# A mixture of experts whose line of experts becomes straight code for one shape, with its first branch a quarter block later

## The chip, the cores and the metric

The kernel runs on one core of a Trainium2 chip. The metric is the device time of one execution in microseconds (us), the median of several runs. TensorE (PE) multiplies, VectorE (DVE) and ScalarE (ACT) move and transform tiles, GpSimd (POOL) starts the indirect transfers (gathers and scatters of rows), and SyncE (SP) starts the plain ones.

## What is computed

Attention with pooled keys and values gives 2304 rows of 512; a dense layer (512 to 2048, square of relu, 2048 to 512) follows; then a layer of 8 experts, which the change is about. Each row goes to the expert with its largest logit:

```python
logits = x @ w_gate
expert_idx = np.argmax(logits, axis=1)
logits_s = logits - logits.max(-1, keepdims=True)
probs = np.exp(logits_s)
probs /= probs.sum(-1, keepdims=True) + 1e-09
gate_w = probs[np.arange(N), expert_idx]
...
h = np.maximum(np.einsum('ecd,edf->ecf', disp, w1), 0.0)
y = np.einsum('ecf,efd->ecd', h, w2)
...
out[i] = gate_w[i] * y[expert_idx[i], pos[i]]
```

Here `disp[e]` holds the rows of expert e, in order, up to its capacity of 576.

## The kernel before

Attention, dense layer and router run in chunks under a written order. Matmuls take float32 as a high and a low part, so a product is three matmuls (high by high, high by low, low by high). The rows of an expert are counted in half blocks of 64 (`nh`), and the experts are sorted by that count, largest first; position r in that order, not the expert's number, names a stage. For this input the counts are 9, 9, 8, 1, 1, 0, 0, 0. All later work hangs on these counts, which are known only on the chip, so each engine reads them from a table (`regs`) into a register and branches on it.

An expert's work is cut into passes. A `pair` takes two blocks of 128 rows: 8 hidden blocks (L1307), then for each block of rows an output block of 24 matmuls (`out_of`, `gb`, L1276), in four quarters of 6 matmuls with a `hook` after each, and then `finish` (ACT scales the rows by their gate, L1254, and POOL scatters them to the output, L1265). A `trio` adds a half block whose high and low parts are stacked (`gb2`, L1282). A `small` pass takes one half block, stacked too: 16 matmuls to the rows `hs[0]`, `hs[1]` (L1414), which ACT (L1419) and DVE (L1421) copy out, 16 to transpose them (L1426), 16 for the output (L1435), and `finish2` (ACT copy L1259, DVE add L1260, ACT scale L1261, scatter L1265). The hooks carry what other engines do for the next pass: the gathers of its rows (`next_rows`, POOL L859), their transposes (`y_trans`, L887, or `y_half`, L904 for one half block; both with an ACT copy and a DVE subtraction), and `w_split`, which turns a 512 KB pair of weight tiles in a staging buffer into high and low parts (ACT L231, DVE L232) and has SP load the next one.

`finish` always goes through one tile `ysb`: ACT may write it only when the scatter before has read it. In `small(1)`, the first small pass, `hs[1]` is that same tile; the tile of `finish2` is `hs[1]` of the second small pass.

The first expert's first pass (`second`) is cut: its first output block runs, then all engines branch on R_LINE (`If` at L1644), and the second output block comes behind the branch in either arm. R_LINE and R_LAST (how many large and small experts follow) are written by 12 small DVE operations in `line_index`. In the arm that this input takes come `trio(0)` and `line(1)`. `line(r)` runs the passes of expert r, a trio or a pair first (`If` at L1578), then a pair; then it branches at L1588 (is there another expert than the last two) and L1589 (is it a large one: `line(r+1)`, or a small one: `smalls(r+1)`). Both branches have joins at which all engines wait for their own work only. `last_two` is two small passes. The order of instructions on PE, DVE and ACT is that of the code. During the last pair of `line`, the third large expert's, `y_trans` 0 to 2 prepare the next rows for either case: whole blocks, and `parted` a half block.

```python
with tc.If(val(regs, R_LAST, 0, NLAST) > (r + 2) // 2):
    with tc.If(halves(r + 1) > 6, preferred_fallthrough_block=False) as on:
        line(r + 1)
    with on.Else():
        smalls(r + 1)
```

Of the kernel before, what the change touches and what calls it, by code (L numbers as in the profile page):

```python
# [26 lines left out]
E = 8  # L27
# [16 lines left out]
R_LAST = R_LINE + 1  # L44
LINE = 4
NLAST = 3
# [153 lines left out]
def tile_kernel(ctx: ExitStack, tc: tile.TileContext, q, k, v, w_in, w_out, w_gate, w1, w2, cap, gate_rows, consts, out):  # L200
# [681 lines left out]
    def y_trans(t=0, then=None):  # L882
# [8 lines left out]
        if then:  # L891
            then(ps)

    def parted(ps):

        for i, t in enumerate(yc):
            nc.scalar.copy(out=t[:, :, 0], in_=ps[:, 2 * i:2 * i + 2, 0:HP])
            nc.vector.tensor_tensor(out=t[:, :, 1], in0=ps[:, 2 * i:2 * i + 2, 0:HP], in1=f(t[:, :, 0]), op=ALU.subtract)

    def y_half():  # L900
        gate_of(0)
        ps = pg.tile([P, KD, HP], F32, tag="g", name="yTs")
        for kk in range(KD):
            nc.tensor.transpose(ps[:, kk, :], got(0)[:HP, kk * P:(kk + 1) * P], ident[:HP, :HP])  # L904
        parted(ps)
# [29 lines left out]
    def early_plan():  # L935
# [3 lines left out]
        def rooms():  # L939
# [10 lines left out]
            st["regs"] = one("regs", [1, R_LAST + 1], I32)  # L950
# [26 lines left out]
    def finalize():  # L977
# [47 lines left out]
        st["nh"], st["cmp"], st["last"] = res[:, 2, 0:E, 0], cmp, ni[:, 0:1]  # L1025

    def line_index():


        nh, least, n, last = st["nh"], st["cmp"], st["ep"][2], st["last"]  # L1030
        for i, x in enumerate((7.0, 2.0, 1.0)):
            nc.vector.tensor_single_scalar(out=least[:, i], in_=nh, scalar=x, op=ALU.is_ge)
        nc.vector.tensor_reduce(out=n, in_=least[:, 0:3], axis=AX.X, op=ALU.add)
        nc.vector.scalar_tensor_tensor(out=last, in0=n[:, 0:1], scalar=2.0, in1=n[:, 2:3], op0=ALU.add, op1=ALU.max)
        nc.vector.tensor_single_scalar(out=regs[:, R_LAST:R_LAST + 1], in_=last, scalar=1, op=ALU.arith_shift_right)
        nc.vector.tensor_tensor(out=n[:, 1:2], in0=n[:, 1:2], in1=n[:, 0:1], op=ALU.is_equal)
        for src, x, op in (
            (nh[:, 0:1], 9.0, ALU.is_equal), (nh[:, 1:2], 9.0, ALU.is_le), (nh[:, 1:2], 7.0, ALU.is_ge),
            (n[:, 2:3], float(2 * NLAST + 1), ALU.is_le),
        ):  # L1040
            nc.vector.scalar_tensor_tensor(out=n[:, 1:2], in0=src, scalar=x, in1=n[:, 1:2], op0=op, op1=ALU.mult)
        nc.vector.scalar_tensor_tensor(
            out=regs[:, R_LINE:R_LINE + 1], in0=st["regse"][:, 2:3], scalar=1.0, in1=n[:, 1:2], op0=ALU.is_ge, op1=ALU.mult
        )
# [192 lines left out]
    yc = [gp.tile([P, 2, 2, HP], F32R, tag="r", name=f"yc{i}", bufs=2) for i in range(2)]  # L1237
    xh, xl = ([gp.tile([P, F2], F32R, tag=tag, name=f"{tag}_e{i}", bufs=2) for i in range(2)] for tag in ("xh", "xl"))
# [18 lines left out]
    def finish2(po, t, sidx, gate):  # L1257
        ot = st["yg2"][:, 0:DM]
        nc.scalar.copy(out=ot[:HP], in_=po[HP:])  # L1259
        nc.vector.tensor_tensor(out=ot[:HP], in0=po[:HP], in1=ot[:HP], op=ALU.add)  # L1260
        nc.scalar.activation(out=ot[:HP], in_=ot[:HP], func=AF.Copy, scale=gate[:HP, t:t + 1])  # L1261
        put(ot, t, sidx, HP)
# [24 lines left out]
    def pair(slot, hooks, extra=0, cut=False):  # L1287
# [39 lines left out]
        if extra:  # L1327
            po = pp.tile([P, 512], F32, tag="y0", name="po2")
            for i in range(4):
                gb2(w, hx, (2 * i, 2 * i + 1), po)  # L1330
                hook(16 + i)
            finish2(po, 2, *sg)
# [9 lines left out]
    def single(slot, hooks):  # L1342
# [44 lines left out]
        po = pp.tile([P, 512], F32, tag="y0", name="po")  # L1387
# [9 lines left out]
    def small(slot, hooks):  # L1397
# [33 lines left out]
        po = pp.tile([P, 512], F32, tag="y0", name="po")  # L1431
# [8 lines left out]
        finish2(po, 0, *sg)  # L1440
# [133 lines left out]
    def line(r):  # L1574


        now = splits(r + 1, {h: [i for i in range(16) if SPLITS[i] == h] for h in range(16)} if r == 1 else W_REST)
        with tc.If(halves(r) > 8, preferred_fallthrough_block=False) as half:  # L1578
            run(trio, r, 0, at=0, extra=now, third=4)
        with half.Else():  # L1580
            run(pair, r, 0, extra=now)
# [4 lines left out]
        if r == LINE:  # L1586
            return
        with tc.If(val(regs, R_LAST, 0, NLAST) > (r + 2) // 2):  # L1588
            with tc.If(halves(r + 1) > 6, preferred_fallthrough_block=False) as on:  # L1589
                line(r + 1)  # L1590
            with on.Else():
                smalls(r + 1)

    def smalls(r):

        small(r % 2, merged(
            {0: [next_rows(r + 1, 1)], 5: [y_half]},
            splits(r + 1, {1: (12, 13), 2: (14, 15)}),
            splits(r + 2, {3: (0, 2), 4: (4, 6, 1), 5: (3, 5), 6: (7, 8, 9), 8: (10, 11)}),
        ))  # L1600
        if r + 2 < 2 * NLAST:
            with tc.If(val(regs, R_LAST, 0, NLAST) > (r + 2) // 2):
                smalls(r + 1)

    def last_two():

        def rows():
            x = val(regs, R_LAST, 0, NLAST, DVE)
            fetch(nc.values_load(regs[0:1, bass.ds(x * (2 * NU) + (2 * E - 1), 1)], engines=DVE, min_val=0, max_val=E * NJ - 1), 1)

        small(1, merged({0: [rows], 5: [y_half]}, {
            h: [lambda i=i: w_split(0, i, None, 0)] for h, i in ((1, 12), (2, 13), (3, 14), (4, 15))
        }))
        small(0, {})
# [28 lines left out]
    with ordered(ET.DVE, ET.Activation):  # L1643
        with tc.If(val(regs, R_LINE, 0, 1) > 0, preferred_fallthrough_block=False) as on:  # L1644
            second()
            run(trio, 0, 1, True, 1, 3, extra={0: [lambda: w_load(regs, 1)]}, third=4)
            line(1)
            last_two()
        with on.Else():
            second()  # L1650
            rest()
# [73 lines left out]
```

## Time and profile before

| What | Value |
|---|---|
| Median of 3 runs | 724.53 us (724.31 to 725.56) |
| Profiled execution, its device time | 725.01 us |
| Its span in the trace | 723.3 us |
| PE busy | 677.9 us (94%) |
| DVE, ACT, POOL busy | 426.3, 330.6, 244.6 us |

The span runs from the first to the last instruction of the profiled execution; 1.7 us of its device time lie outside. Times in the trace are counted from the span's start. The first output block of the experts ends at 540 us, so the experts take about the last quarter of the span. A share of busy time is an average over all stages. A row of the timeline gives start, duration, engine, line, operation, output and input, and in brackets the engine's idle time before it and what ended it ("issue": nothing that the profile shows; PEldq and PEq are PE's sequencer, which runs ahead of its matmuls).

### The profile page before, as it was taken

What the parts mean: (1) busy time and instruction counts of PE and PEld (TensorE: products, weight loads), DVE (VectorE), ACT (ScalarE), POOL (GpSimd) and SP (SyncE); (2) the same over time, 40 slices, a digit from 0 to 9 for tenths busy, and PEclk for the clock granted to TensorE, in tenths of its full rate; (3) what the DMA queues carried; (4) which work ended last, traced back from release to release, by engine and by line L of the source; (5) the groups of instructions that cost most, each with busy time, mean ns of one, the idle gap of its engine ahead of it and who ended that gap; (6) DMA issues with size and microseconds to landing.
All of it is one profiled execution on the core that took longest, in us unless ns stands there. A gap on an engine that the chain in (4) does not pass through costs nothing. (4 is left out here: it accounts for less than half of the span.)

```text
span 723.3 us, 12144 instructions
## 1 busy us (share of the span) xinstructions
PE 677.9 (94%) x4223; PEld 595.8 (82%) x4224; DVE 426.3 (59%) x1131; ACT 330.6 (46%) x941; POOL 244.6 (34%) x265
## 2 busy tenths in 40 slices
PE   3799999999999999999999999989988999999965
PEld 3668888898878988888988898888877898998854
DVE  6899799321399894382597294245462746552621
ACT  3878777344434334444244244244412646542522
POOL 4578899232253223243223233222121120222111
PEclk9899999999999999999999999999999999999989
DMA  9979911300412300000010000440016647272430
GB/s 329 404 271 328 274 34 45 120 24 15 161 30 63 97 29 9 21 32 15 2 45 16 1 30 1 145 148 1 30 44 242 197 149 245 70 259 75 142 114 4
DMA packets 42238, 77.09 MB, mean 107 GB/s; under 512 B 8609, under 2 KB 18081, under 8 KB 42016
## 3 DMA queue, kind: packets, MB, share of 16 engines
q1 hardware_dynamic: 39472, 67.51, 27.4%
q0 software_dynamic: 2672, 8.46, 3.8%
q8 instruction: 42, 0.69, 0.4%
q14 instruction: 52, 0.43, 0.2%
HBM read 63.05 MB, written 13.18 MB: 105 GB/s over the span
## 5 line engine op out<-in xcount | busy, mean ns | idle before, releaser
L592 PE MATMUL h<-xh,W 128*128 128x256 f32 x1152 | 216.5, 286 | 4.6 <-DVE r L604 3.4
L612 POOL TENSOR_TENSOR gl<-r,gh 128x256 fp32r<-128x256 f32 x144 | 119.5, 832 | 266.4 <-ACT gh L608 181.9
L592 PEld LDWEIGHTS h<-xh,W 128*128 128x128 f32 x1152 | 184.2, 190 | 16.8 <-DVE r L604 4.7
L625 PE MATMUL y<-W,gh 128*128 128x512 f32 x576 | 186.1, 404 | 0.3 <-POOL W L281 0.3
L592 PE MATMUL h<-xl,W 128*128 128x256 f32 x576 | 162.3, 282 | 0.0
L604 DVE SCALAR_TENSOR_TENSOR r<-h,r 128x256 f32<-128x256 f32 x141 | 59.0, 418 | 107.9 <-ACT r L597 107.6
L625 PE MATMUL y<-W,gl 128*128 128x512 f32 x288 | 113.8, 395 | 0.0
L625 PEld LDWEIGHTS y<-W,gh 128*128 128x128 f32 x576 | 98.7, 189 | 17.2 <-issue 1.9
L592 PEld LDWEIGHTS h<-xl,W 128*128 128x128 f32 x576 | 109.7, 190 | 0.0
L597 ACT ACTIVATE r<-h 128x256 f32<-128x256 f32 x144 | 55.0, 382 | 113.9 <-PE h L592 98.0
L608 ACT CAST gh<-r 128x256 fp32r<-128x256 f32 x144 | 58.5, 406 | 92.4 <-DVE r L604 87.5
L1307 PE MATMUL hp<-yh,W 128*128 128x256 f32 (+1 forms) x384 | 74.6, 291 | 0.1
L274 DVE SCALAR_TENSOR_TENSOR cv<-raw,cv 128x512 int32<-128x512 int32 x64 | 70.1, 1118 | 0.0
L1276 PE MATMUL po<-W,xh_e 128*128 128x512 f32 x192 | 62.5, 407 | 5.5 <-issue 5.5
L682 DVE SCALAR_TENSOR_TENSOR junk<-ysb,wgb 128x512 bf16<-128x512 f32 x80 | 66.3, 828 | 1.6
L625 PEld LDWEIGHTS y<-W,gl 128*128 128x128 f32 x288 | 54.1, 188 | 13.9 <-POOL gl L612 1.2
L1307 PEld LDWEIGHTS hp<-yh,W 128*128 128x128 f32 x384 | 61.1, 188 | 0.9 <-DVE xl_e L1313 0.3
L1307 PE MATMUL hp<-yl,W 128*128 128x256 f32 (+1 forms) x192 | 55.7, 290 | 0.0
L1265 POOL DMA_INDIRECT out_dram<-ysb,sidx x14 | 13.8, 987 | 118.3 <-ACT ysb L1254 94.2
L281 POOL TENSOR_TENSOR W<-cv,W 128x512 fp32r<-128x512 f32 x32 | 48.9, 1534 | 9.0 <-ACT W L278 9.0
L232 DVE TENSOR_TENSOR W<-stg,W 128x512 fp32r<-128x512 f32 x64 | 42.4, 687 | 5.7 <-ACT W L231 4.9
L521 PE MATMUL av<-aT,vz 128*128 128x256 f32 (+3 forms) x192 | 42.6, 354 | 3.4 <-DVE xl L531 2.3
(201 smaller groups left out, 909.1 us busy)
## 6 DMA issues: line engine op xcount, KB each, us to landing
stg<-in_moe_w_dram SPq DMA_DIRECT2D x45, 512.0 KB, 4.9
raw<-in_moe_w_in_dram SPq DMA_DIRECT2D x16, 512.0 KB, 7.9
raw<-in_moe_w_out_dram SPq DMA_DIRECT2D x16, 512.0 KB, 8.0
kraw<-in_k_dram SPq DMA_DIRECT2D x16, 288.0 KB, 3.0
out_dram<-zt SPq DMA_DIRECT2D x18, 256.0 KB, 4.2
y_dram<-ysb SPq DMA_DIRECT2D x18, 256.0 KB, 2.2
qT<-in_q_dram SPq DMA_DIRECT2D x16, 256.0 KB, 2.6
vraw<-in_v_dram SPq DMA_DIRECT2D x16, 256.0 KB, 3.0
```

The costliest lines, as they stand in the source:

```text
L274: nc.vector.scalar_tensor_tensor(out=a, in0=box["raw"][:, :, 1], scalar=x, in1=a, op0=op, op1=ALU.bitwise_or)
L281: nc.gpsimd.tensor_tensor(out=W[i][:, 1], in0=f(box["a"]), in1=f(W[i][:, 0]), op=ALU.subtract)
L521: nc.tensor.matmul(ps[:, :n], vz[:m, cm].rearrange("p r d -> p (r d)"), abox["aT"][:m, blk, :n], start=(x == 0), stop=(x == 1),)
L592: nc.tensor.matmul(ps, wt[kk][:, l, o:o + P], r[:, kk, :], start=(n == 0), stop=(n == 3 * KD - 1))
L597: nc.scalar.activation(out=box["r"], in_=box["ps"], func=AF.Relu)
L604: nc.vector.scalar_tensor_tensor(out=r, in0=box["ps"], scalar=0.0, in1=r, op0=ALU.max, op1=ALU.mult)
L608: nc.scalar.copy(out=box["gh"], in_=box["r"])
L612: nc.gpsimd.tensor_tensor(out=box["gl"], in0=box["r"], in1=f(box["gh"]), op=ALU.subtract)
L625: nc.tensor.matmul(st["y", c][t], l[:, ts], r, start=(ff == 0 and n == 0), stop=(ff == NF - 1 and n == 2))
L682: nc.vector.scalar_tensor_tensor(out=junk, in0=st["yb", c, t] if c < 2 else st["ysb", c][t], scalar=1.0, in1=st["wgb"][:, e], op0=ALU.mult ...
L1276: nc.tensor.matmul(ps, l, r, start=(fi == 0 and x == 0), stop=(fi == 7 and x == 2))
L1307: nc.tensor.matmul(ps, ww[:, l, o], r[:, kk, 0:n2], start=(kk == 0 and x == 0), stop=(kk == KD - 1 and x == 2))
```

## The change

The line of experts becomes straight code for one shape: three large experts (the first has 9 half blocks, the second and third are a trio or a pair and a pair), and two small ones behind them. R_LINE now asks for just that (nh of positions 0 to 5), R_LAST and the branches at L1588 and L1589 are gone, and `line_index` has 5 operations. The branch at L1578 on each large expert remains. The cut of the first pass moves: one quarter of the second output block (6 matmuls) runs ahead of the branch, and what follows (`rest_of`) begins with the transposes of the next rows. In the last pair only one half block is gathered and transposed (`y_half`), so `parted` is gone from `y_trans`. `finish2` of the small passes works in two halves of 256 columns. `small(1)` now splits its remaining tiles through `splits(4, W_REST)`, which loads two more 512 KB pairs of a further expert's weights that nobody uses. The output tiles `py` are made once.

```diff
     def line_index():
-        nh, least, n, last = st["nh"], st["cmp"], st["ep"][2], st["last"]
-        for i, x in enumerate((7.0, 2.0, 1.0)):
-            nc.vector.tensor_single_scalar(out=least[:, i], in_=nh, scalar=x, op=ALU.is_ge)
-        nc.vector.tensor_reduce(out=n, in_=least[:, 0:3], axis=AX.X, op=ALU.add)
...
-        nc.vector.scalar_tensor_tensor(
-            out=regs[:, R_LINE:R_LINE + 1], in0=st["regse"][:, 2:3], scalar=1.0, in1=n[:, 1:2], op0=ALU.is_ge, op1=ALU.mult
-        )
+        nh, n = st["nh"], st["ep"][2]
+        src = st["regse"][:, 2:3]
+        for i, x, op in ((0, 9.0, ALU.is_equal), (1, 9.0, ALU.is_le), (2, 7.0, ALU.is_ge), (3, 1.0, ALU.is_le), (5, 0.0, ALU.is_le)):
+            out = n[:, 1:2] if i < 5 else regs[:, R_LINE:R_LINE + 1]
+            nc.vector.scalar_tensor_tensor(out=out, in0=nh[:, i:i + 1], scalar=x, in1=src, op0=op, op1=ALU.mult)
+            src = out
-    def finish2(po, t, sidx, gate):
-        ot = st["yg2"][:, 0:DM]
-        nc.scalar.copy(out=ot[:HP], in_=po[HP:])
-        nc.vector.tensor_tensor(out=ot[:HP], in0=po[:HP], in1=ot[:HP], op=ALU.add)
-        nc.scalar.activation(out=ot[:HP], in_=ot[:HP], func=AF.Copy, scale=gate[:HP, t:t + 1])
+    def finish2(po, t, sidx, gate, parts=1):
+        ot, n = st["yg2"][:, 0:DM], DM // parts
+        cols = [slice(i * n, i * n + n) for i in range(parts)]
+        for c in cols:
+            nc.scalar.copy(out=ot[:HP, c], in_=po[HP:, c])
+            nc.vector.tensor_tensor(out=ot[:HP, c], in0=po[:HP, c], in1=ot[:HP, c], op=ALU.add)
+        for c in cols:
+            nc.scalar.activation(out=ot[:HP, c], in_=ot[:HP, c], func=AF.Copy, scale=gate[:HP, t:t + 1])
         put(ot, t, sidx, HP)
-        def out_of(t):
-            po = pp.tile([P, 512], F32, tag=f"y{t}", name=f"po{t}")
-            for i in range(4):
-                gb(w, hh, hl, t, (2 * i, 2 * i + 1), po)
-                hook(8 + 4 * t + i)
-            finish(po, t, *sg)
-        out_of(0)
-        if cut:
-            return lambda: out_of(1)
-        out_of(1)
+        def out_of(t, parts=range(4), cut=False):
+            for i in parts:
+                gb(w, hh, hl, t, (2 * i, 2 * i + 1), py[t])
+                if cut:
+                    return
+                hook(8 + 4 * t + i)
+            finish(py[t], t, *sg)
+        def rest_of():
+            hook(12)
+            out_of(1, range(1, 4))
+        out_of(0)
+        out_of(1, cut=cut)
+        if cut:
+            return rest_of
-    def line(r):
...
-        pair(r % 2, merged(
-            {0: [next_rows(r + 1, 3)], 8: [lambda: y_trans(0, parted)], 9: [lambda: y_trans(1)], 10: [lambda: y_trans(2)]},
-            splits(r + 2, W_LATE),
-        ))
...
+    def line():
+        for r in (1, 2):
+            now = splits(r + 1, {h: [i for i in range(16) if SPLITS[i] == h] for h in range(16)} if r == 1 else W_REST)
+            with tc.If(halves(r) > 8, preferred_fallthrough_block=False) as half:
+                run(trio, r, 0, at=0, extra=now, third=4)
+            with half.Else():
+                run(pair, r, 0, extra=now)
+            rows = {8: [lambda: y_trans(0)], 9: [lambda: y_trans(1)], 10: [lambda: y_trans(2)]} if r == 1 else {8: [y_half]}
+            pair(r % 2, merged({0: [next_rows(r + 1, 3 if r == 1 else 1)]}, rows, splits(r + 2, W_LATE)))
+        small(1, merged({0: [next_rows(4, 1)], 5: [y_half]}, splits(4, W_REST)))
         small(0, {})
```

On PE the program at the first branch reads as follows before, from the last matmuls of the first output block (`po_6407`; the names are of output, weight and activation tiles) to the first of the second, whose rows stand here in the order of both arms.

```order
L1276 MATMUL po_6407<-W_1375,xh_e_6133 128x512 x2
L1276 MATMUL po_6407<-W_1375,xl_e_6135 128x512
L850 TENSOR_LOAD regs
L1644 COMPARE_AND_BRANCH
L1276 MATMUL po_12060<-W_911,xh_e_6132 128x512 x2
L1276 MATMUL po_12060<-W_911,xl_e_6134 128x512
L1276 MATMUL po_12060<-W_963,xh_e_6132 128x512 x2
L1276 MATMUL po_12060<-W_963,xl_e_6134 128x512
L887 MATMUL yTp<-cst,yg 128x128 x4
```

The same place after the change, where `po_6133` is the second output block.

```order
L1263 MATMUL po_6132<-W_1375,xh_e_6135 128x512 x2
L1263 MATMUL po_6132<-W_1375,xl_e_6137 128x512
L1263 MATMUL po_6133<-W_911,xh_e_6134 128x512 x2
L1263 MATMUL po_6133<-W_911,xl_e_6136 128x512
L1263 MATMUL po_6133<-W_963,xh_e_6134 128x512 x2
L1263 MATMUL po_6133<-W_963,xl_e_6136 128x512
L847 TENSOR_LOAD regs
L1607 COMPARE_AND_BRANCH
L884 MATMUL yTp<-cst,yg 128x128 x4
```

Six matmuls have moved ahead of the register load and the branch (now L847 and L1607), and the first work behind it is the transposes of the gathered rows.

On DVE the end of `line_index` before, from the indices of the next rows (`cur`) to the branch; two comparisons of L1032 stand further ahead.

```order
L871 TENSOR_SCALAR cur<-idxt 128x3
L1032 TENSOR_SCALAR cmp<-res 1x8
L1033 TENSOR_REDUCE erf<-cmp 1x3
L1034 SCALAR_TENSOR_TENSOR ni<-erf 1x1
L1036 TENSOR_TENSOR erf<-erf 1x1
L1035 TENSOR_SCALAR regs<-ni 1x1
L1041 SCALAR_TENSOR_TENSOR erf<-res,erf 1x1 x3
L1041 SCALAR_TENSOR_TENSOR erf<-erf 1x1
L1042 SCALAR_TENSOR_TENSOR regs<-regse,erf 1x1
L850 TENSOR_LOAD regs
L1644 COMPARE_AND_BRANCH
```

After the change, at the same place; two operations of L1026 stand further ahead.

```order
L868 TENSOR_SCALAR cur<-idxt 128x3
L1026 SCALAR_TENSOR_TENSOR erf<-res,erf 1x1 x2
L1026 SCALAR_TENSOR_TENSOR regs<-res,erf 1x1
L847 TENSOR_LOAD regs
L1607 COMPARE_AND_BRANCH
```

Between the indices and the write of the condition nine operations are left out but for three.

On ACT the end of the last pair and the start of the first small pass before (`W` are weight tiles, `stg` staging buffers, `ha` the product that `hs[0]` is copied from).

```order
L231 CAST W_1046<-stg_5445 128x512
L1254 ACTIVATE ysb_8_6123<-po_10562,gate 128x512
L1589 UNCONDITIONAL_BRANCH
L1588 UNCONDITIONAL_BRANCH x2
L1602 UNCONDITIONAL_BRANCH
L1588 UNCONDITIONAL_BRANCH x2
L1602 UNCONDITIONAL_BRANCH x2
L1588 UNCONDITIONAL_BRANCH x2
L1419 COPY ysb_8_6122<-ha_11924 128x512
```

And after the change.

```order
L228 CAST W_1046<-stg_5445 128x512
L1238 ACTIVATE ysb_8_6123<-po_6133,gate 128x512
L1410 COPY ysb_8_6122<-ha_8781 128x512
L228 CAST W_1250<-stg_5446 128x512
L228 CAST W_1290<-stg_5446 128x512
L1419 ACTIVATE xl_e_6137<-hT_8816 128x4x64
```

The branches between `finish` of the last pair and the first small pass are gone; nothing else has moved there.

## Rows read from the trace of the kernel before

**Rows 1.** Page: the span and its instructions.
```profile
span 723.3 us, 12144 instructions
```

**Rows 2.** Waits, 540 to 723: engine, operation, releaser: total us, times, longest.
```profile
PE ha L1414 <- ACTq L1588: 7.3, 1, 7.3
...
PE po L1276 <- issue: 5.5, 2, 4.1
```

**Rows 3.** Timeline, DVE and PE, first branch.
```profile
536.90 0.15 DVE L1032 TENSOR_SCALAR cmp<-res 1x8 f32<-1x8 f32 x1
...
538.26 0.15 DVE L1042 SCALAR_TENSOR_TENSOR regs<-regse,erf 1x1 int32<-1x1 int32 x1
...
544.27 1.22 PE L1276 MATMUL po<-W,xh_e 128*128 128x512 f32 x2 [4.07 <-issue]
...
549.19 0.63 PE L1276 MATMUL po<-W,xh_e 128*128 128x512 f32 x2 [1.47 <-issue]
```

**Rows 4.** Source L850, 534 to 540: ns min/median/max, first and last start.
```profile
L850 PEldq EVENT_SEMAPHORE  x6: 51/51/2215, 535.9 to 538.6; - x6
```

**Rows 5.** Source L1644, 530 to 545, the same columns.
```profile
L1644 PEldq COMPARE_BRANCH  x1: 4908/4908/4908, 539.3 to 539.3; - x1
```

**Rows 6.** Windows: us; PE, PEld, DVE, ACT, POOL busy (instructions); PE clock; DMA share; GB/s.
```profile
544.30:547.00 2.70, 2.70 (x6) 2.02 (x7) 0.00 (x0) 0.00 (x0) 0.00 (x0) 0.50 1.01 244
...
658.40:662.30 3.90, 3.90 (x18) 3.19 (x18) 0.00 (x0) 0.00 (x0) 0.89 (x1) 1.00 0.19 71
...
471.90:475.60 3.70, 3.67 (x18) 3.67 (x19) 1.42 (x3) 1.96 (x5) 1.46 (x2) 0.54 0.21 82
```

**Rows 7.** Source L1578, the whole span.
```profile
L1578 PEldq COMPARE_BRANCH  x3: 69/352/3777, 581.1 to 658.5; - x3
```

**Rows 8.** Source L1588, 680 to 696.
```profile
L1588 PEldq COMPARE_BRANCH  x3: 188/193/6543, 682.8 to 690.0; - x3
```

**Rows 9.** Timeline, last pair to the end.
```profile
679.14 0.46 PE L887 MATMUL yTp<-cst,ysb 64*128 64x64 f32 x4
...
682.24 1.04 POOL L1265 DMA_INDIRECT out_dram<-ysb,sidx  x1 [12.34 <-ACT ysb L1254]
...
686.30 0.40 PE L1276 MATMUL po<-W,xl_e 128*128 128x512 f32 x1
690.16 0.69 ACT L1254 ACTIVATE ysb<-po,gate 128x512 f32<-128x512 f32 x1 [5.58 <-DMA out_dram<-ysb,sidx]
691.12 1.00 POOL L1265 DMA_INDIRECT out_dram<-ysb,sidx  x1 [7.84 <-ACT ysb L1254]
...
693.95 5.57 PE L1414 MATMUL ha<-W,yc 128*128 128x512 f32 x16 [7.25 <-ACTq L1588]
...
699.56 0.69 DVE L1421 COPY ysb<-ha 128x512 f32<-128x512 f32 x1
...
705.70 3.87 PE L1414 MATMUL ha<-W,yc 128*128 128x512 f32 x16
705.95 0.58 ACT L1259 COPY ysb<-po 64x512 f32<-64x512 f32 x1 [2.16 <-PE po L1435]
...
711.35 1.11 PE L1426 MATMUL hT<-cst,ysb 128*128 128x64 f32 x8 [0.94 <-DVE ysb L1421]
...
717.57 0.72 ACT L1261 ACTIVATE ysb<-ysb,gate 64x512 f32<-64x512 f32 x1 [0.75 <-DVE ysb L1260]
```

**Rows 10.** DMA issues, 679.4 to 685.4: queue, count, KB, us to landing.
```profile
stg<-in_moe_w_dram SPq DMA_DIRECT2D x6, 512.0 KB, 6.3
out_dram<-ysb,sidx POOLq DMA_INDIRECT x1, 7.8
```

**Rows 11.** DMA issues, 691.0 to 691.2.
```profile
out_dram<-ysb,sidx POOLq DMA_INDIRECT x1, 3.5
```

**Rows 12.** Timeline, 552.9 to 553.9: copy and subtraction of 256 columns.
```profile
553.00 0.37 ACT L889 CAST yh<-yTp 128x256 fp32r<-128x256 f32 x1 [1.20 <-PE yTp L887]
553.41 0.42 DVE L890 TENSOR_TENSOR yl<-yTp,yh 128x256 fp32r<-128x256 f32 x1 [0.82 <-ACT yh L889]
```

More of the change, by code (lines that the diff above doesn't have):

```diff
@@ L43 @@
 R_LINE = R_MAX + 1
-R_LAST = R_LINE + 1
-LINE = 4
-NLAST = 3
 NSTG = 7
@@ L880, in gate_of, with y_trans @@
         nc.vector.tensor_copy(out=st["gt"][:, t:t + 1], in_=got(t)[:, DM:DM + 1])
-    def y_trans(t=0, then=None):
+    def y_trans(t=0):
         gate_of(t)
@@ L890, in y_trans @@
         nc.vector.tensor_tensor(out=st["yl"][:, :, o], in0=ps, in1=f(st["yh"][:, :, o]), op=ALU.subtract)
[L891 to L898, printed above, removed]
     def y_half():
@@ L904, in y_half @@
             nc.tensor.transpose(ps[:, kk, :], got(0)[:HP, kk * P:(kk + 1) * P], ident[:HP, :HP])
-        parted(ps)
+        for i, t in enumerate(yc):
+            nc.scalar.copy(out=t[:, :, 0], in_=ps[:, 2 * i:2 * i + 2])
+            nc.vector.tensor_tensor(out=t[:, :, 1], in0=ps[:, 2 * i:2 * i + 2], in1=f(t[:, :, 0]), op=ALU.subtract)
     def w_part(e, i):
@@ L949, in rooms @@
             st["gt"] = one("gt", [P, 3])
-            st["regs"] = one("regs", [1, R_LAST + 1], I32)
+            st["regs"] = one("regs", [1, R_LINE + 1], I32)
             st["regse"] = one("regse", [1, 3], I32)
@@ L1024, in finalize @@
         nc.vector.tensor_copy(out=regs[:, R_MAX:R_MAX + 1], in_=nbf[:, 0:1])
-        st["nh"], st["cmp"], st["last"] = res[:, 2, 0:E, 0], cmp, ni[:, 0:1]
+        st["nh"] = res[:, 2, 0:E, 0]
     def line_index():
-        nh, least, n, last = st["nh"], st["cmp"], st["ep"][2], st["last"]
-        for i, x in enumerate((7.0, 2.0, 1.0)):
-            nc.vector.tensor_single_scalar(out=least[:, i], in_=nh, scalar=x, op=ALU.is_ge)
-        nc.vector.tensor_reduce(out=n, in_=least[:, 0:3], axis=AX.X, op=ALU.add)
[L1034 to L1041, printed above, removed]
-        nc.vector.scalar_tensor_tensor(
-            out=regs[:, R_LINE:R_LINE + 1], in0=st["regse"][:, 2:3], scalar=1.0, in1=n[:, 1:2], op0=ALU.is_ge, op1=ALU.mult
-        )
+        nh, n = st["nh"], st["ep"][2]
[4 more added lines that the diff above has]
+            src = out
     units = [(0, i) for i in range(LEAD)]
@@ L1237, in tile_kernel @@
     yc = [gp.tile([P, 2, 2, HP], F32R, tag="r", name=f"yc{i}", bufs=2) for i in range(2)]
+    py = [pp.tile([P, 512], F32, tag=f"y{t}", name=f"po{t}") for t in range(2)]
     xh, xl = ([gp.tile([P, F2], F32R, tag=tag, name=f"{tag}_e{i}", bufs=2) for i in range(2)] for tag in ("xh", "xl"))
@@ L1314, in pair @@
             hook(fi)
-        def out_of(t):
-            po = pp.tile([P, 512], F32, tag=f"y{t}", name=f"po{t}")
-            for i in range(4):
-                gb(w, hh, hl, t, (2 * i, 2 * i + 1), po)
-                hook(8 + 4 * t + i)
-            finish(po, t, *sg)
-        out_of(0)
-        if cut:
-            return lambda: out_of(1)
-        out_of(1)
-        if extra:
-            po = pp.tile([P, 512], F32, tag="y0", name="po2")
-            for i in range(4):
-                gb2(w, hx, (2 * i, 2 * i + 1), po)
+        def out_of(t, parts=range(4), cut=False):
[12 more added lines that the diff above has]
+            return rest_of
+        if extra:
+            for i in range(4):
+                gb2(w, hx, (2 * i, 2 * i + 1), py[0])
                 hook(16 + i)
-            finish2(po, 2, *sg)
+            finish2(py[0], 2, *sg)
     def trio(slot, hooks):
@@ L1386, in single @@
         hook(3)
-        po = pp.tile([P, 512], F32, tag="y0", name="po")
+        po = py[0]
         gb(w, hp, lp, 0, (0, 1), po)
@@ L1430, in small @@
             hook(3 + half)
-        po = pp.tile([P, 512], F32, tag="y0", name="po")
+        po = py[0]
         for i in range(4):
@@ L1439, in small @@
             hook(5 + i)
-        finish2(po, 0, *sg)
+        finish2(po, 0, *sg, 2)
     def merged(*ds):
@@ L1572, in tile_kernel @@
     W_REST = {1: (12,), 2: (13,), 3: (14,), 4: (15,)}
-    def line(r):
[L1577 to L1581, printed above, removed]
-        pair(r % 2, merged(
-            {0: [next_rows(r + 1, 3)], 8: [lambda: y_trans(0, parted)], 9: [lambda: y_trans(1)], 10: [lambda: y_trans(2)]},
-            splits(r + 2, W_LATE),
-        ))
[L1586 to L1613, printed above, removed]
+    def line():
[8 more added lines that the diff above has]
+        small(1, merged({0: [next_rows(4, 1)], 5: [y_half]}, splits(4, W_REST)))
         small(0, {})
@@ L1646, in tile_kernel @@
             run(trio, 0, 1, True, 1, 3, extra={0: [lambda: w_load(regs, 1)]}, third=4)
-            line(1)
-            last_two()
+            line()
         with on.Else():
```

## The prediction

> **What bounds the kernel now.** The span is 723.3 us [rows 1] and PE is busy for 94% of it, so the change can win only where PE stands still, or where the chain behind the last matmul is long. I read the waits of the experts' part first [rows 2], then the timeline around each wait [rows 3, 9], then the sequencers' rows there. Two waits stand out. The reader is to see that they have different ends.
>
> The first is PE's stop at the first branch. PE ends its first output block at 540.20 (544.27 − 4.07) and starts again at 544.27 [rows 3]. Its sequencer runs ahead: it came to the wait for the condition at 535.9, 4.3 us before the array was done, and stood there for 2.2 us [rows 4]. DVE wrote the condition at 538.26 to 538.41 [rows 3]; 0.9 us later, at 539.3, the branch began, and it took 4.91 us [rows 5]: 539.3 + 4.91 = 544.2, which is PE's start, and the longest of PE's waits that name no releaser [rows 2]. So the end of the stop is condition plus 0.9 plus 4.91, and PE's own end has no part in it. The stop costs more than itself: the six matmuls behind it ran for 2.70 us at a granted clock of 0.50 [rows 6], the lower of the two levels, and after the transposes PE stood 1.47 us more [rows 3], again with no releaser.
>
> The second is the join at L1588: PE ends at 686.70 (686.30 + 0.40) and starts at 693.95 [rows 9], 7.3 us for which the waits name ACT's sequencer [rows 2]. PE's own branch took 6.54 us, but from 682.8 [rows 8], so it was over at about 689.4. What ACT waits for is the scatter of the block before: issued at 682.24 [rows 9], it took 7.8 us [rows 10], with six weight loads of 512 KB in flight, and landed at 690.05. Then ACT scales the last block (690.16 to 690.85) and POOL scatters it from 691.12 [rows 9]; ACT's branches take the rest up to 693.95, 3.1 us. PE then ran its 16 matmuls in 5.57 us, where the same 16 of the second small pass took 3.87 [rows 9].
>
> **The first branch, part by part.** `line_index` loses operations. Nine ran from 536.90 to 538.41 [rows 3], 0.17 us each; three are left there, so the condition is written at 537.40. With the same 0.9 the branch begins at 538.3. PE has six more matmuls ahead of it; at 3.87/16 = 0.24 us each [rows 9] that is 1.4 us. Its sequencer comes to the wait at 535.9 + 1.4 = 537.3, just before the condition, so it hides nothing of the move. The branch takes 4.91 as before and ends at 543.2; the array ends at 540.20 + 1.4 = 541.6. PE stands for 1.6 us instead of 4.07. Behind the branch come the transposes (about 0.4 us), done at 543.6. Before, the same work (six matmuls and the transposes) was over, with the second stop, at 549.19 [rows 3]. The gain is 5.6 us if nothing stops PE there again and the clock holds. Neither is sure: the 1.47 us stop, of which I see no releaser, is likely to be there still, since the code behind the branch is as far away; and a stop of 2.14 us was followed by 3.7 us at a clock of 0.54 [rows 6], which on that stretch is 1.3 to 1.7 us, while one of 0.94 [rows 9] was not. I take one of the two: 5.6 − 1.5 = 4.1 us. The bounds: 0, if PE restarts 4.07 us after its own last matmul whatever it is, with all that follows; 6.7, if the branch takes 3.78 us, which is what the one at L1578 took [rows 7]. That one cost nothing: PE was busy for 3.90 of 3.90 us across it [rows 6], because as much work was queued. Here the six matmuls are cover of 1.4 us, and the gain of the move alone lies there.
>
> [...]
>
> **The join.** In the frame of before's times, PE goes from 686.70 right into `small(1)`. Transposes become fewer: three sets of 0.46 us [rows 9] or a little more become one; on PE they overlap with their neighbours, and I take 0.8 us off, so that PE ends the pair at 685.9. ACT and DVE also have three fewer copies or subtractions each in that pair, of 0.4 us [rows 12] to 0.7, so that weight splits, and with them the loads, come 1.4 to 2.2 us earlier, and the first scatter some 0.9 earlier, at 681.3. With the loads gone earlier it should take about 6.6 us instead of 7.8 and land at 687.9. ACT scales the last block to 688.7, POOL scatters at 688.9, and that takes 3.5 us as before [rows 11]: 692.35. There the old wait comes back in another place: `hs[1]` of `small(1)` is the tile that this scatter reads. The matmuls ahead of it (3.87 us) are done at 689.8, so PE stands about 2.2 to 2.5 us, for DVE's copy at 692.35. Before, the copy at 699.56 was followed by `finish2` at 705.95 [rows 9], 6.4 us later; now that is 698.75. The gain is 7.2 us, and as the stop may bring the lower clock (half of 1.4), I take 6.5. The bounds: 3.3 where the first scatter lands no earlier (the second at 694.6, `finish2` at 701.0, 5.0 gained, less 1.7 for the clock, which is 5.57 − 3.87); 9.3 where it takes only the 3.5 us of an undisturbed one (copy at 690.3).
>
> **`finish2` in halves.** Copy 0.58 and scale 0.72 [rows 9] and the add between them (0.75 with its gap) are serial. In halves a copy is about 0.37 and an add 0.42 [rows 12]: copy, add, add, scale come to 0.37 + 0.42 + 0.42 + 0.45 with gaps, against 2.05. That is 0.37 at the end, where it is all on the path, and as much at the change from the first small pass to the second, where PE waits 0.94 us for DVE's copy [rows 9], which waits for that scatter. Together 0.7, from 0.3 (only the end) to 1.0.
>
> **At nothing.** Two loads more in `small(1)`: its staging comes free as the splits go, so they are issued behind its hidden matmuls and land some microseconds before its scatter. If they collide with it the scatter takes up to 7.8 instead of 3.5 us, and the second small pass waits up to 4 us; its PE stop of 0.94 would show it. The smaller R_LINE and output tiles made once move no instruction on a waiting engine.
>
> **The sum.** 4.1 + 6.5 + 0.7 = 11.3 us. Against the profiled execution: 725.01 − 11.3 = 713.7. That execution is 0.48 over the median, so 713.2 us for the median.
>
> **Rivals.**
> - The first branch gives nothing, because what PE waits for is its queue's refill after its own end. For it: the idle names no releaser. Against it: the times add up to the condition plus the branch. 724.53 − 7.2 = 717.3.
> - The join's wait is that of the scatters, and moves whole into `small(1)`; the branches themselves are cheap. For it: ACT's 5.58 us wait for the DMA [rows 9]; it is what is left if the first scatter stays at 690.05 and the second takes up to 7.8. Gain at the join 3.3 down to 1.1, so 716.4 to 718.6. [...]
> - Slower: the code comes late at the jumps that stay (into and out of the arms at L1578). With PE's queue as long as 3.9 us, a jump of 6.54 would leave 2.6 us of idle and 1.3 to 1.7 of clock, about 4.2 each. Three such (12.6) outweigh the 11.3: the time would be 726. Against it: all three compare-and-branch rows at L1578 together cost PE nothing before, and those jumps keep the same work ahead of them.
> - The condition is false and the general arm runs. Against it: two small passes of 16 matmuls [rows 9] behind three large experts are the shape that is asked for. If so, over 730.
>
> **Chances.** The forecast and what lies around it 0.72; the first branch nothing 0.13; the scatters 0.09; slower by the jumps 0.04; the other arm 0.01; the rest is no change. A measurement of this kernel tells about 0.2%, 1.4 us, from no change. Faster 0.93, same 0.02, slower 0.05. With all bounds low the gain is 3.6 (720.9), with all high 17.0 (707.5). These together are unlikely; 708.5 to 719.0 takes in the first two rivals and leaves 2 in 10 out.
>
> **What would show it.** Right: PE's stop at the first branch of 1 to 2 us, the branch still 4 to 5 us long but begun about 1 us earlier; no stop of PE with a sequencer as releaser at the end of the last pair, but one of 1.5 to 3 us before the transposes of `small(1)`, with DVE's copy of `hs[1]` waiting for the scatter; the last copy, add and scale 0.3 to 0.4 us shorter. Wrong: a first stop of 4 us again; a scatter of 7 us or more between the last pair and `small(1)`; PE idle inside the passes of the second and third expert, behind a jump.

## The result

The changed kernel takes 713.44 us (median of 4 runs, 711.94 to 714.38), the kernel before 725.0 on the same chip (724.31 to 725.56): a ratio of 0.9836 (95% interval 0.9818 to 0.9854), 11.6 us faster. The forecast was 713.2 in a range of 708.5 to 719.0. The total was right; its terms were not all.

The profiled execution took 711.94 us. Its page, and PE's waits from the first expert on (engine, operation, releaser: total us, times, longest):

```profile
span 710.2 us, 12047 instructions
...
PE hT L1417 <- DVE ysb L1412: 2.7, 2, 1.6
PE yTp L884 <- issue: 1.2, 1, 1.2
PE hp L1294 <- issue: 1.2, 1, 1.2
```

The 7.3 us for ACT's sequencer [rows 2] are gone. In their place stands a wait for DVE's copies in the small passes. Two waits of 1.2 us name no releaser: the first branch's (`yTp`), and a new one in the second expert (`hp`). The first branch in PE's and DVE's timeline, and in the rows of PE's sequencer:

```profile
535.70 0.15 DVE L1026 SCALAR_TENSOR_TENSOR regs<-res,erf 1x1 int32<-1x1 f32 x1
...
539.62 0.39 PE L1263 MATMUL po<-W,xl_e 128*128 128x512 f32 x1
...
541.25 0.63 PE L884 MATMUL yTp<-cst,yg 128*128 128x128 f32 x4 [1.25 <-issue]
541.63 0.71 PE L1263 MATMUL po<-W,xh_e 128*128 128x512 f32 x2
```
```profile
L847 PEldq EVENT_SEMAPHORE  x6: 51/51/51, 535.7 to 536.3; - x6
```
```profile
L1607 PEldq COMPARE_BRANCH  x1: 4137/4137/4137, 536.9 to 536.9; - x1
```

No wait on a semaphore is longer than 51 ns now: the condition (535.85) is there when the sequencer comes. The branch takes 4.14 us instead of 4.91 [rows 5]. The stop is 1.25 us, not 4.07 [rows 3], and no second stop follows. The end of the last pair and the first small pass:

```profile
675.02 1.01 POOL L1252 DMA_INDIRECT out_dram<-ysb,sidx  x1 [14.02 <-ACT ysb L1238]
...
679.32 3.89 PE L1405 MATMUL ha<-W,yc 128*128 128x512 f32 x16
...
680.99 0.69 ACT L1238 ACTIVATE ysb<-po,gate 128x512 f32<-128x512 f32 x1 [3.63 <-PE ha L1405]
681.57 0.58 ACT L1410 COPY ysb<-ha 128x512 f32<-128x512 f32 x1
681.95 1.01 POOL L1252 DMA_INDIRECT out_dram<-ysb,sidx  x1 [1.62 <-ACT ysb L1238]
...
684.90 0.69 DVE L1412 COPY ysb<-ha 128x512 f32<-128x512 f32 x1 [1.50 <-DMA out_dram<-ysb,sidx]
...
685.64 1.10 PE L1417 MATMUL hT<-cst,ysb 128*128 128x64 f32 x8 [1.60 <-DVE ysb L1412]
...
692.70 0.37 ACT L1245 COPY ysb<-po 64x256 f32<-64x256 f32 x1 [3.15 <-PE po L1426]
693.10 0.42 DVE L1246 TENSOR_TENSOR ysb<-po,ysb 64x256 f32<-64x256 f32 x1 [3.23 <-ACT ysb L1245]
693.55 0.37 ACT L1245 COPY ysb<-po 64x256 f32<-64x256 f32 x1 [0.48 <-DVE ysb L1246]
693.83 1.09 ACT L1248 ACTIVATE ysb<-ysb,gate 64x256 f32<-64x256 f32 x2
```

PE goes from the last pair straight into the 16 matmuls, where [rows 9] have 7.25 us of idle, and stands 1.60 us later, at `hs[1]`, for the scatter, as forecast. The last rows show what was not: the copy of the second half waits for the add of the first. The clock of three stretches, in windows with the columns of [rows 6]: behind the first branch and into the small pass it is 1.00, behind the small pass's stop 0.75, and in windows of 1 us there 0.50 from 688 to 690 and 1.00 from 691 on. These are the two levels of this trace: of 600 windows of 0.5 us, 400 to 700, 592 have 1.00, 6 have 0.50 and 2 lie between (570, 24 and 6 before).

```profile
541.20:543.20 2.00, 1.95 (x11) 1.66 (x12) 0.00 (x0) 0.52 (x1) 0.00 (x0) 1.00 0.96 256
679.40:683.00 3.60, 3.60 (x17) 2.92 (x16) 0.30 (x1) 2.01 (x4) 1.93 (x2) 1.00 1.05 412
685.60:692.50 6.90, 6.86 (x29) 5.29 (x30) 3.28 (x8) 1.43 (x4) 0.00 (x0) 0.75 0.56 152
```

To set this against the sum, I cut every kernel's trace at four ends of PE's matmuls, read off its rows as start plus duration: the first output block, the last pair, the first small pass, the last matmul. What lies ahead of the first cut is the same work in all of them and yet moves (it ends at 540.20 before and 538.64 after, and between 537.2 and 541.1 in the runs below), so the stages show more than the medians. But each trace is one execution, and those of one kernel differ by up to 7 us (e2: 712.50 to 719.21, and its trace is of the longest; that of e1 is of its shortest, 712.54 of 712.54 to 718.79). The kernel before, run beside the others, had medians of 725.2 to 725.8. By the intervals of the ratios to it, e3, e9 and e12 are slower and e7 and e10 faster than the changed kernel; time alone does not tell the others from it.

| Kernel | block to last pair | to end of first small pass | to PE's end | median |
|---|---|---|---|---|
| before | 146.50 | 19.16 | 10.34 | 725.0 |
| changed | 140.84 | 13.13 | 10.52 | 713.44 |
| e1, no quarter | 144.34 | 11.63 | 10.53 | 715.57 |
| e2, late condition | 143.69 | 15.01 | 10.52 | 714.80 |
| e3, both | 146.18 | 14.63 | 10.52 | 719.29 |
| e4, near join | 139.73 | 14.28 | 10.49 | 714.10 |
| e5, whole last step | 140.91 | 12.95 | 10.36 | 711.45 |
| e6, no extra loads | 140.82 | 11.87 | 10.53 | 713.28 |
| e7, rows elsewhere | 140.74 | 12.00 | 9.43 | 708.47 |
| e8, two quarters | 139.24 | 15.16 | 10.53 | 711.56 |
| e9, far join | 140.33 | 19.35 | 10.54 | 718.38 |
| e10, best | 139.15 | 10.07 | 9.50 | 706.15 |
| e11, transposes back | 141.34 | 16.16 | 10.50 | 714.84 |
| e12, quarter alone | 142.86 | 20.52 | 10.36 | 722.30 |

From before to after: 5.66 + 6.03 − 0.18 = 11.5 us behind the first block, and 1.6 ahead of it, which the change does not touch: 13.1, the difference of the spans. The traced execution of the changed kernel is its fastest, 1.5 us under its median, so the medians differ by 11.6.

### The profile page after: what moved, and what is told of

Its sections match the earlier page's. It is cut to its first block, busy times and chain, and to the rows that moved or that the text cites. A ratio compares the mean times of both kernels' runs of the same rounds, so it can differ in the third digit from the quotient of the medians.

```text
span 710.2 us, 12047 instructions
## 1 busy us (share of the span) xinstructions
PE 674.1 (95%) x4215; PEld 592.9 (83%) x4216; DVE 424.3 (60%) x1119; ACT 330.1 (46%) x940; POOL 241.5 (34%) x263
```

## The experiments

**The first branch** (e1, e2, e3 undo parts of it; e8 goes on; e12 does one part alone).

e1, the branch right behind the first block:

```diff
-        out_of(1, cut=cut)
         if cut:
-            return rest_of
+            return lambda: out_of(1)
+        out_of(1)
```

> The changed kernel with one part undone: the first branch stands again right behind the first output block, with no quarter block ahead of it; the short condition stays. My theory (PE's stop ends when the condition is written, plus about 1 us, plus a branch of 4.1 to 4.9 us, and PE's own end has no part in it): the branch still begins about 1.05 us after the condition is written, ends about 541.0 if the stages before keep the times of the profile after, and PE, done 1.4 us earlier, stands 2.4 to 2.7 us instead of 1.25. From the end of the first output block to the end of the first quarter and the first transposes 4.4 us instead of 3.0, or about 5.7 if the lower clock follows the stop, and 1.5 more if the second stop returns: 1.4 to 4.2 us slower than the changed kernel. Rival (the stop is a fixed time behind PE's own last matmul, as if the queue had to be refilled): 4.1 us of stop as before, and 9 us over that stretch: 6 us slower.

Condition, stop and branch:

```profile
534.29 0.15 DVE L1026 SCALAR_TENSOR_TENSOR regs<-res,erf 1x1 int32<-1x1 f32 x1
...
540.05 1.09 PE L1263 MATMUL po<-W,xh_e 128*128 128x512 f32 x2 [2.80 <-issue]
```
```profile
L1607 PEldq COMPARE_BRANCH  x1: 4652/4652/4652, 535.3 to 535.3; - x1
```

The condition is written at 534.44, the branch begins 0.9 later, takes 4.65 and ends at 539.95; PE starts at 540.05. A stop of 2.80 where 2.4 to 2.7 was expected and 4.1 by the rival; then the clock was 0.54 from 540 to 543. From the end of the block to the end of the first quarter and transposes it takes 6.1 us, where 3.0 are the changed kernel's and 9 the rival's. The first stage is 3.5 us longer. The total by the three stages is 2.0 longer, because in the first small pass the clock held (1.00 from 687.7 to 693.2).

e2, six more small operations ahead of the condition:

```diff
-... (3, 1.0, ALU.is_le), (5, 0.0, ALU.is_le)):
+... *((3, 1.0, ALU.is_le),) * 7, (5, 0.0, ALU.is_le)):
```

> The changed kernel with six more small DVE operations ahead of the write of the condition (one factor of it, repeated), so that it is written about as late as before. My theory: the condition comes 6 x 0.165 = 1.0 us later, the branch begins and ends 1.0 us later, and PE's stop grows from 1.25 to about 2.2 us: 1.0 us slower than the changed kernel, 2.4 if the lower clock follows. Rival (PE's sequencer, which comes to the wait only at 535.7, sets the start of the branch, and the condition is early enough): no change of the stop, same time.

The same rows of this kernel:

```profile
539.24 0.15 DVE L1026 SCALAR_TENSOR_TENSOR regs<-res,erf 1x1 int32<-1x1 f32 x1
...
544.88 0.96 PE L884 MATMUL yTp<-cst,yg 128*128 128x128 f32 x4 [2.43 <-issue]
```
```profile
L1607 PEldq COMPARE_BRANCH  x1: 4435/4435/4435, 540.3 to 540.3; - x1
```

Condition 539.39, branch 540.3, end 544.7: the stop is 2.43, 1.2 us longer, and the lower clock follows (0.52 from 544.9 to 548). The first stage is 2.85 us longer: the condition set the end, as my theory said.

e3, both edits.

> Both at once, so that of the changed kernel only the straight line, the shorter last pair and the halves remain. My theory: a stop of 3.4 to 4.1 us, the lower clock behind it, and perhaps the second stop: 2.4 to 6 us slower than the changed kernel, so 716 to 719.5 us, and 5.5 to 9 us faster than before; the stretch from the end of the first output block to the end of the first transposes comes near the 9 us of before. Rival (the straight line also mends the first branch, since its arm is shorter and lies nearer): no lower clock, no second stop, and not more than 2.4 us slower than the changed kernel.

The stop is 3.71 us and the clock behind it 0.50 (540.8 to 543.8). From the end of the block to the end of the first quarter and transposes it takes 7.1 us, against 3.0 in the changed kernel and 9.0 before: these two parts carry 4.2 of the 6.0 us. The second stop did not come back; in that the rival was right. That the stage of 146.18 is nearly that of before (146.50) is partly chance, since PE stands 1.58 us at the branch of the second expert:

```profile
582.53 0.56 PE L1294 MATMUL hp<-yh,W 128*128 128x320 f32 x2 [1.58 <-ACT ysb L1245]
```
```profile
L1570 PEldq COMPARE_BRANCH  x1: 5390/5390/5390, 577.1 to 577.1; - x1
```

The wait is put down to ACT, but it ends with PE's own branch: 577.1 + 5.39 = 582.5. In e1 it is the same (5.30 us, and a stop of 1.50); in the changed kernel that row takes 0.36.

e8, two quarters ahead:

```diff
-                if cut:
+                if cut and i:
                     return
...
             hook(12)
-            out_of(1, range(1, 4))
+            hook(13)
+            out_of(1, range(2, 4))
```

> The changed kernel with two quarters of the second output block ahead of the first branch instead of one, and two sets of transposes behind it at once. My theory (with the quarter moved, PE's sequencer comes to the wait just when the condition is ready, so from now on every matmul moved ahead of the branch delays the branch as much as it covers): the branch begins 1.4 us later against the same condition, and PE's stop is 1.0 to 1.3 us as now: within 0.3 us of the changed kernel. Rival (what is moved ahead of the branch covers it one for one): no stop, 1.2 us faster.

The branch began at 538.1 instead of 536.9 and took 4.00; the stop was 1.12 us. A second quarter covers nothing more, as expected. The stage is 1.6 us shorter all the same; 1.2 of it is the new stop in the second expert, which is not there (why stays open).

e12, the kernel before with the quarter alone (its `out_of`, `rest_of` and `py` are the change's).

> The kernel before with only the quarter block moved ahead of the first branch; its long condition and its line stay. My theory (the stop ends with condition plus branch, here as late as before): the condition ends PE's stop at the same place, and 1.4 us of the 4.07 are covered: a stop of 2.5 to 2.8 us; the second stop of 1.5 us stays, since what follows the branch is as before. 1.4 us faster than before, or up to 3 us if the lower clock falls on less work. Rival (the quarter alone brings what the changed kernel has at the first branch): no second stop, no lower clock, 4 to 6 us faster.

The stop is 2.44 us, as expected, but neither a second stop nor a lower clock followed (1.00 from 542.1 to 545.1). The ratio to before is 0.9957 (0.9941 to 0.9973), 3.1 us: more than the 1.4 that the move covers, less than the rival's 4 to 6, though the rival was right about the stop and the clock. The first stage is 3.6 us shorter than before, the second 1.4 longer, with the old join at 7.67 us of idle instead of 7.25.

**The join** (e4 and e9 put one back, e11 puts gathers and transposes back).

e4 and e9, a branch whose arm this input never enters, so that every engine jumps over it:

```diff
+        with tc.If(halves(3) > 1):
+            small(1, {})                    # e4
+            for i in range(15):             # e9, in its place
+                pair(i % 2, {})
         small(1, merged({0: [next_rows(4, 1)], 5: [y_half]}, splits(4, W_REST)))
```

> The changed kernel with one branch put back ahead of the first small pass: its arm holds a small pass that this input never takes, so the work is the same. My theory (at a join PE cannot go on before ACT has come there, ACT waits for the scatter, and the branch costs on top): PE stands 4 to 7 us between the last pair and the first small pass, with ACT's sequencer or its own branch ahead of it, the stop at the copy of hs[1] shrinks or goes, and the kernel is 3 to 6 us slower than the changed one. Rival (the scatters alone set the time, and the branch is hidden or cheap): the stop only moves from the copy of hs[1] to the join; less than 1.5 us slower.

> The changed kernel with one branch put back ahead of the first small pass, as in the run with the near join, but with an arm of 15 untaken pairs, so that each engine jumps about as far as it did before. My theory (in the kernel before, PE waited 3.1 us after ACT's scale of the last block because ACT had to jump far; with the near arm this was 0.2 us): ACT comes out of the branch 2.5 to 3.5 us after its scale, PE stands 5 to 6 us instead of 2.6, and from the end of the last pair to the end of the first small pass there are 16.5 to 18 us instead of 14.3: 2.5 to 3.5 us slower than with the near arm. Rival (the distance costs nothing, the join before was long only because the scatter landed late and the joins were nested): as with the near arm, 14 to 14.5 us.

The sequencers' rows at the branch, near and far:

```profile
L1576 PEldq COMPARE_BRANCH  x1: 241/241/241, 675.2 to 675.2; - x1
...
L1576 ACTq COMPARE_BRANCH  x1: 50/50/50, 681.2 to 681.2; - x1
L1576 ACTq EVENT_SEMAPHORE  x1: 17/17/17, 681.6 to 681.6; - x1
```
```profile
L1576 PEldq COMPARE_BRANCH  x1: 6447/6447/6447, 677.2 to 677.2; - x1
...
L1576 ACTq COMPARE_BRANCH  x1: 50/50/50, 684.2 to 684.2; - x1
...
L1576 ACTq EVENT_SEMAPHORE  x1: 17/17/17, 687.2 to 687.2; - x1
```

PE and ACT around it, near and then far:

```profile
680.84 0.69 ACT L1238 ACTIVATE ysb<-po,gate 128x512 f32<-128x512 f32 x1 [3.87 <-DMA out_dram<-ysb,sidx]
...
681.69 5.34 PE L1405 MATMUL ha<-W,yc 128*128 128x512 f32 x16 [2.60 <-ACTq L1576]
```
```profile
683.95 3.96 PE L1405 MATMUL ha<-W,yc 128*128 128x512 f32 x16 [2.89 <-PEq L1576]
...
687.40 0.59 ACT L1410 COPY ysb<-ha 128x512 f32<-128x512 f32 x1 [2.88 <-ACTq L1576]
...
691.14 1.11 PE L1417 MATMUL hT<-cst,ysb 128*128 128x64 f32 x8 [1.99 <-DVE ysb L1412]
...
695.28 0.66 PE L894 MATMUL yTs<-cst,yg 64*128 64x64 f32 x4 [1.35 <-DMA yg<-y_dram,gix]
```

With the near join PE stands 2.60 us for ACT, and the stop at `hs[1]` is gone: the rival's reading, 1.15 us more than the changed kernel. With the far arm PE's own branch takes 6.4 us and ACT comes out 3.0 us after its own; the stage is 19.35 us, that of before (19.16). The size was my theory's and above it; the place was not: PE did not stand 5 to 6 us at the join. It went on after 2.89, ahead of ACT's branch at 684.2, and then waited 1.99 for DVE's copy of `hs[1]` and 1.35 for a gather (`yg`), which POOL issues only at 690.57 (679.34 in the changed kernel). The sequencers' rows show the price of the far jump: 6.45 us against 0.24 on PE, and on ACT 3.0 against 0.4 from its branch to its next row. How much of the 5.1 us between the two runs it makes is not shown, for two other things differ: the first scatter took 7.1 us (6.1 with the near arm, 5.9 in the changed kernel), and the arms differ in kind, a small pass and pairs.

e11, `y_trans` 0 to 2 and `parted` in the last pair again:

```diff
-            rows = {8: [lambda: y_trans(0)], 9: [lambda: y_trans(1)], 10: [lambda: y_trans(2)]} if r == 1 else {8: [y_half]}
+            rows = {8: [lambda r=r: y_trans(0, parted if r == 2 else None)], 9: [lambda: y_trans(1)], 10: [lambda: y_trans(2)]}
-            pair(r % 2, merged({0: [next_rows(r + 1, 3 if r == 1 else 1)]}, rows, splits(r + 2, W_LATE)))
+            pair(r % 2, merged({0: [next_rows(r + 1, 3)]}, rows, splits(r + 2, W_LATE)))
```

> The changed kernel with the three gathers and three sets of transposes, with their copies, back in the last pair. My theory (they hold PE for 0.8 us and put the weight loads and with them the first scatter of that pair off): the pair takes 0.8 us more, the first scatter lands about 1 to 1.7 us later against the pair's end, PE's stop at the copy of hs[1] is 2.5 to 3.5 us instead of 1.6, and the kernel is 1.5 to 3 us slower than the changed one. Rival (the scatter goes by the loads that are issued anyway, and lands as it does now): only the 0.8 us.

The first scatter took 7.5 us instead of 5.9, and landed 3.0 us after the pair's end instead of 1.4. ACT was late with `hs[0]` too (a stop of 0.68), then 2.16 us at `hs[1]`. The stages are 0.5 and 3.0 us longer; by the ratio to before (0.9862 against 0.9836) it is 1.9 us, with intervals that overlap.

**The small passes.** e5, the last step whole:

```diff
-        finish2(po, 0, *sg, 2)
+        finish2(po, 0, *sg)
```

> The changed kernel with the last step of the small passes whole again, one copy, add and scale of 512 columns. My theory after the profile (the copy of the second half waits for the add of the first, so the halves run one behind the other and gain nothing): from the copy's start to the scatter 2.33 us as before instead of 2.49, and PE's stop in the second small pass 0.94 instead of 1.11: 0.15 to 0.35 us faster than the changed kernel, which the time alone can hardly tell. Rival (the halves overlap, as the prediction had it): 0.4 us longer at the end, 0.7 us slower in all.

The step of the second small pass in the timeline:

```profile
702.77 0.58 ACT L1245 COPY ysb<-po 64x512 f32<-64x512 f32 x1 [3.37 <-PE po L1426]
703.39 0.68 DVE L1246 TENSOR_TENSOR ysb<-po,ysb 64x512 f32<-64x512 f32 x1 [3.52 <-ACT ysb L1245]
704.10 0.72 ACT L1248 ACTIVATE ysb<-ysb,gate 64x512 f32<-64x512 f32 x1 [0.75 <-DVE ysb L1246]
705.10 0.91 POOL L1252 DMA_INDIRECT out_dram<-ysb,sidx  x1 [9.39 <-POOLq L1607]
```

From copy to scatter 2.33 us; in halves it was 705.66 − 703.17 = 2.49. The second stop fell from 1.11 to 0.94. The halves cost 0.3 us in all, which the medians cannot tell.

e6, the first small pass's splits without loads:

```diff
-        small(1, merged({0: [next_rows(4, 1)], 5: [y_half]}, splits(4, W_REST)))
+        small(1, merged({0: [next_rows(4, 1)], 5: [y_half]}, {h: [lambda i=i: w_split(0, i, None, 0)] for h, (i,) in W_REST.items()}))
```

> The changed kernel without the two extra weight loads in the first small pass (its splits stay). My theory: nothing; both loads land 3 us before that pass scatters its rows, and its scatter takes 2.2 us already: within 0.2 us. Rival (they share the queues with the scatter that the copy of hs[1] waits for): that stop of 1.6 us shrinks, 0.5 to 1.5 us faster.

713.28 us, and the same waits: the stop at `hs[1]` is 1.81, not shorter than 1.60, so the rival fell. Its shorter second stage (11.87) goes with the clock, which held at 1.00 behind that stop.

e7, `hs[1]` in another tile:

```diff
-        hs = rows_h(slot)
+        hs = rows_h(slot)[0], st["yg"][:, 1, 0:DM]
```

> The changed kernel with hs[1] of both small passes in a tile that no scatter reads (the unused second half of the gathered rows), so that DVE's copy waits for the matmuls alone. My theory (PE's stops of 1.6 and 1.1 us in the small passes are the wait for the scatters, and the low clock behind the first comes from the stop): both stops fall under 0.5 us, the clock holds through the first small pass, and from the end of the last pair to the end of the first small pass there are 10.2 to 10.8 us instead of 13.1: 3.5 to 4.5 us faster than the changed kernel, about 709.5. Rival (the clock falls there for another cause, as power or the loads): only the two stops go, 2.2 to 2.7 us faster. Second rival (ACT, held by the same scatter for the last block, is late with hs[0] and what follows): less than 1 us faster.

The stops fell to 0.9 (ACT's `hs[0]`, behind the scale that waits for the first scatter) and 0.7, the clock held (1.00 from 678.6 to 700), and the stage is 12.00, not 10.2 to 10.8: the second rival had a part. With 9.43 in the last stage and 708.47 us (ratio 0.9779, 0.9743 to 0.9815) it is 5 us under the changed kernel by the medians; 2.2 us of that are in these two stages, and the rest lies ahead of the first block or between the executions.

e10, all of it: the last block goes out through the unused tile, so ACT waits no more either; last step whole, no extra loads, two quarters (the edits of e5, e6 and e8, not shown again).

```diff
-        ot = st["ysb", NCH - 1][1]
+        ot = st["yg"][:, 1, 0:DM] if t and st.get("last") else st["ysb", NCH - 1][1]
...
-        hs = rows_h(slot)
+        hs = (rows_h(1) if slot else (rows_h(0)[0], st["yg"][:, 1, 0:DM]))
```

> A version from what the runs pointed to: the last block of the last pair goes out through the unused half of the gathered rows, so that neither ACT's scale nor the copies of the small passes wait for a scatter, the last step is whole, the two extra loads are gone, and two quarters stand ahead of the first branch. My theory: no stop of PE over 0.5 us from the last pair to the end but for the transposes that wait for the copies of their own pass; from the end of the last pair to the end of the first small pass 10.2 to 11 us instead of 13.1, to the end of PE's work 9.3 instead of 10.5, 0.15 less at the end, and the stop of 1.2 us in the second expert may be gone as in the run with two quarters: 4.5 to 6 us faster than the changed kernel, 707 to 709. Rival (the scatter of the last block and the loads delay the weights of the first small pass instead): not more than 4 us faster.

PE, from the last pair to its end, in two windows:

```profile
676.60:686.90 10.30, 10.30 (x54) 8.38 (x53) 4.74 (x10) 4.64 (x10) 1.99 (x2) 1.00 0.43 160
686.90:696.40 9.50, 9.46 (x48) 7.58 (x46) 2.35 (x6) 2.66 (x5) 0.91 (x1) 1.00 0.02 5
```

PE does not stop (busy for 10.30 of 10.30 and 9.46 of 9.50 us), and the clock holds (1.00 in both). 706.15 us, ratio 0.9736 (0.9718 to 0.9754): 19 us under before and 7 under the change by the medians, where 4.5 to 6 was expected; by the three stages it is 5.8 under the change.

## Why the prediction was right, and where it was not

**First branch, 4.1 forecast.** The mechanism held in each of five kernels (before, e1, e2, e3, e12): condition, 0.9 us, a branch of 4.4 to 4.9 us, and PE's own end without a part. In the changed kernel PE's sequencer comes just when the condition does, and in e8 after it (at 536.8, when DVE had read the written condition at 535.6), so that its arrival takes the condition's place. From the end of the block to the end of the first quarter and transposes before took 549.19 − 540.20 = 9.0 us and now 3.0: 6.0 us. The step that was mis-sized is "I take one of the two", 1.5 us: neither the second stop nor the lower clock came (1.00 from 541.2 to 543.2). That the second stop hangs on the distance of the code behind the branch, as the forecast had it, no run shows: e12 keeps the line of before and has no such stop. The rest is the branch, put at 4.91 "as before", which took 4.14. Against it, 1.2 us are lost in the second expert, which the forecast did not have. The rival that nothing is gained is excluded by e1 and e3.

**The join, 6.5 forecast with the transposes.** 6.0 in the stage, and ahead of it 0.5 by e11. The forecast's chain stands in the rows: scatter, scale, scatter, `hs[1]`, a stop of 1.6 us where "about 2.2 to 2.5" was said, and a lower clock behind it (0.75 from 685.6 to 692.5). What it did not separate is why the old stop was long. e4 and e9 bear on it: with one branch put back the stage is 1.2 us longer with a near target and 6.2 with a far one. The second rival's cheap branch is that of the near target. The far one is not cheap, and its 3.0 us on ACT are about the 3.1 that the prediction had from ACT's scale to PE's start; that the nesting of the old joins had no part is not shown. The near branch took 241 ns on PE and 50 on ACT, the far one 6447 on PE and again 50 on ACT, whose 3.0 us lie behind its row. The rows show these durations; why a far jump takes that long, they do not show.

**`finish2` in halves, 0.7 forecast.** Measured −0.16 from the copy to the scatter at the end, and −0.18 in the last stage of PE's work: the step "copy, add, add, scale" failed, because the second copy waits for the first add. Why it waits, no run shows.

**At nothing:** the two loads cost nothing that e6 shows. **Jumps that stay:** the prediction named PE idle inside the second expert's passes, behind a jump, as a sign of being wrong, and 1.19 us of it are there; that the jump makes them is not shown. In e1 and e3 a jump does (1.50 and 1.58 us). It was far from the 4.2 us each of this rival, and "slower" did not come.

That the total was met to 0.3 us is luck: +1.9 at the branch, −1.0 at the halves and −1.2 in the second expert nearly cancel.

## What to carry to other kernels

Ask of a branch on a value from the chip how far its target lies and how much work the engine has queued, and take both from the sequencer's rows; here a far jump (e9) took 3.0 us on ACT and its row 6.45 on PE, a near one (e4) 0.4 and 0.24, and moving work ahead of a branch covered it only until the sequencer itself came later than the condition (a stop of 1.25 us with one quarter, 1.12 with two). When a join goes, look for the buffer that the next stage shares with a transfer in flight: here the wait came back there (1.60 us at `hs[1]`), and tiles that no transfer in flight reads (e10, with the clock at 1.00) took 4.1 us out of the two small passes, 0.3 of it by the whole last step. Do not count on splitting a serial chain over two engines before a row shows that the halves overlap; here they did not (ACT's second copy stood 0.48 us for DVE's first add).

## What was not expected of the hardware

A stop of the same length is sometimes followed by the lower clock and sometimes not: 2.43 us by 0.52 (e2), 2.44 by 1.00 (e12); 1.53 by 0.60 (e3, 689.4 to 698.0), 1.57 by 1.00 (e1, 687.7 to 693.2), 1.81 by 1.00 (e6). With nearly the same stop and the same instructions, the stage of the first small pass takes 14.63 us in e3 and 11.63 in e1; what decides it stays open. Open too is the stop of about 1.2 us in the second expert, which names no releaser, and is there in the changed kernel, e2, e5, e6, e7 and e9 (1.05 to 1.33), shorter in e11 (0.60), e12 (0.30) and e4 (0.16), and not in before, e8 and e10; and the second stop of before, which went with the quarter alone (e12) and with the straight line without the quarter (e3).
